# A hand-planned attention and gated-MLP kernel on one core: the order of its steps is made anew under another port rule, with small shifts for every head pair

## The chip, the core and the metric

The kernel runs on one core of a Trainium2 chip. The metric is the device time of one execution in microseconds; the number compared is the median of repeated runs.

## What is computed

```python
# q, k, v: (8, 12, 448, 64); w_in: (768, 1024); conv_w: (3, 1024); w_out: (1024, 768)
q_n, k_n = rmsnorm(q, g_q), rmsnorm(k, g_k)            # over the last axis
attn = softmax(q_n @ k_n.T / 8)                        # per batch and head
x = (attn @ v).transpose(0, 2, 1, 3).reshape(8, 448, 768)
h = relu(x @ w_in)
conv = sum(conv_w[i] * shifted(h, i - 1) for i in range(3))   # along the sequence
out = (h * sigmoid(conv)) @ w_out
```

The weights arrive in a 64-bit format, so the kernel converts them first. Products that need more than half precision are split: a value becomes an f16 part ("hi") and the f16 rest ("lo"), and three f16 products replace one f32 product.

## The kernel before, in words

The unit of attention is a pair of heads of one batch; there are 48 pairs, n = 0 to 47, six to a batch. A pair has three parts. `plan_qk` loads q and k, makes squares and sums, takes the inverse root (`rsqrt`, nine tiny steps), scales, turns the result on TensorE and splits it into hi and lo; `q_middle` copies a corner of qT into a zero-padded tile `qz` for the one row group that does not fill a pair. `plan_attention` makes the scores in four groups (`scores`, L685), their row maxima (`soft_max`, L691), the exponentials on ScalarE (`soft_exp`, L700), the f16 split of the exponentials (`p_hi`, `p_lo`, tile `ph`), a turn by DMA (`p_turn`, tile `PT`), the product with v (`pv`, L836) and the scaled result x (`x_scale`, `x_hi`, `x_lo`). `plan_v` loads v and finds its scale. From pair 10 on v is split too: `v_hi` on ScalarE or VectorE and `v_lo` (L813, tile `vp`) on VectorE alone. After six pairs the batch has its x, and `plan_moe` runs the first product (`in_part`, L910), relu, convolution (`in_conv`, L938), tanh, gate (L948), the split of the gated rows (`in_hi`, `in_lo`, tile `gring`) and the second product (`out_part`, L989).

None of this is issued loop by loop. Every step is entered with a due time, `at(t, fn, ...)`. The due times come from `base(n)`, the planned start of pair n (T0 per pair for the first N0 pairs, T after that), and from other constants of the table `PH`. A list scheduler in the program, run while the kernel is built, then picks one step after the other for PE, DVE, ACT, POOL and SP. It has a cost for each step and engine (`options`), the order that buffers force (`needs`), and an urgency made from the due times. For steps with two possible engines `PH` has a patience: how long the second engine in the list is held back. The steps are issued in the order in which the scheduler picked them, and each engine runs its steps strictly in that order; the real waits are on semaphores for data and buffers. The plan's times do not exist on the chip, only the order, the choice of engines and of PSUM banks.

VectorE and GpSimd share a port. The scheduler has a list of VectorE steps that use it (`SHARED`: `p_lo`, `p_hi`, `v_lo`, `in_lo`, `q_middle`, `in_carry`, `rsqrt`, `convert` and others); all GpSimd steps use it. Its rule for them in the kernel before is symmetric, where `port[e]` is the end of the last such step on engine e:

```python
elif locks(e, step[0], *step[1:2]):
    t = max(t, port["POOL" if e == "DVE" else "DVE"] - PH["pk"])      # pk = 0.1
key = t + sw + (BETA if e != "SP" else PH["sp"]) * urgency(step), urgency(step), steps[step][1]
```

Of the five engines' picks the one with the earliest t is issued next.

Of the kernel before, what the change touches and what calls it, by code (L numbers as in the profile page):

```python
# [17 lines left out]


PH = dict(  # L20
    T0=11.0, N0=5, T=16.382, ti=26.404, si=4.968, so=8.925, hop=0.57, beta=0.03, wi0=-36.475,
    wi1=117.871, wo0=26.473, wo1=139.734, cw=-9.12, tg=-82.146, tl=35.844, ea=1.04, te=111.609,
    ep=0, hs=0, nf=3, adj=0.195, nz=8, ne=0, sc=5, tc=2, mc=8, p_qe=0.915, p_evac=0.829,
    p_hi=1.187, p_lo=6.193, p_rms=1.564, p_v=0.867, p_x=0.08, p_g=2.103, p_relu=0.547,
    p_cv=1.109, p_qz=0.74, p_ev=6.084, sp=0.156, nbulk=8, p_rs=0.048, p_sq=0.882, p_w=0.552,
    v0=-6.388, dg=7, n1=10, sw=0.0, nl=4, tj=-0.029, hk=0, pvs=1, pk=0.1, p_sa=0.11, p_ph=0.44,
    p_pl=0.718, nq=3, nk=94, p_qh=0.371, p_ql=0.382, tq=10.598, ti0=0.047, ti1=0.203, ti2=-0.226,
    ti3=0.674, ti4=0.066, ti5=0.097, ti6=0.664, ti7=0.034, si0=0.995, si1=1.598, si2=1.683,
    si3=1.424, si4=1.546, si5=1.144, si6=1.904, si7=0.784, to0=0.237, to1=0.332, to2=-0.03,
    to3=0.013, to4=0.104, to5=-0.691, to6=-0.117, to7=0.351, so0=1.431, so1=1.535, so2=1.849,  # L30
    so3=1.519, so4=2.105, so5=1.499, so6=1.215, so7=0.981,
)
SCHED = {}
ON_ACT = ""
# [20 lines left out]
def tile_attention_moe(ctx: ExitStack, tc, q, k, v, g_q, g_k, w_in, conv_w, w_out, out):  # L55
# [6 lines left out]
    B, H, S, D = q.shape  # L62
# [3 lines left out]
    NPAIR = B * NP  # L66
# [1 line left out]
    NT = S // 64  # L68
    NO2 = DM // 2
    PSC = 2.0 ** 14  # L70
    T = PH["T"]

    def base(n):

        return min(n, PH["N0"]) * PH["T0"] + max(n - PH["N0"], 0) * T

    def queue(kind):
        return nc.scalar if kind in ON_ACT.split() else nc.sync
# [18 lines left out]
    def move(e, dst, src):  # L97
# [8 lines left out]
    BUFS = dict(  # L106
        qkf=2, sq=2, st=2, qT=2, kT=2, qz=2, v=4, sst=6, e=2, PT=2, x=10, c=2, o=1,
        rB=1, vacc=2, vsc=4, cwb=3, s=PH["sc"], t=PH["tc"], m=PH["mc"], rd=2, rsum=2, rT=1, mx=10, ph=3, vp=2,
    )
# [44 lines left out]
    plan = []  # L154

    def at(t, fn, *args):
        plan.append((t, len(plan), fn, args))
# [13 lines left out]
    cw = const.tile([P, 3, NFC], F32, name="cw")  # L171
    wi32 = const.tile([P, DM // P + 1, DFF], F32, name="wi32")
    wo32 = const.tile([P, NFC + 1, DM], F32, name="wo32")
# [76 lines left out]
    free_i = wo32.rearrange("p c e -> p (c e)").bitcast(I32)  # L250
    free_o = gring.rearrange("p n w t -> p (n w t)").bitcast(I32)
# [161 lines left out]
    def duo(n):  # L413

        return (n, 1) if n < 2 else (n - n % 2, 2)
# [136 lines left out]
        e.tensor_copy(z[HALF[h], :, HALF[h]], old("qT", n)[HALF[h], :, t0 : t0 + 64])  # L552

    def plan_qk(n):
        s = base(n)
        lead = PH["tl"] if n else 60.0
        if duo(n)[0] == n:
            at(s - lead, load_k, n)
            at(s - lead, load_q, n)
        at(s - 24.0, square, n)  # L560
        if halved(n):
            at(s - 23.0, square_half, n)
        at(s - 22.0, square_sum, n)
        if duo(n)[0] == n:
            for i in range(NRS):
                at(s - 20.0 + 0.3 * i, rsqrt, n, i)
        for i in (1, 0):
            at(s - 15.0 - i, apply_rms, n, i)
            if turned(n, i):
                if i:  # L570
                    at(s - 14.5 - i, apply_gain, n)
                at(s - PH["tq"] - 3.0 - i, x_cast, n, i)
                at(s - PH["tq"] - 2.0 - i, x_rest, n, i)
                at(s - PH["tq"] - i, x_turn, n, i)
                continue
            at(s - 10.0 - i, qk_transpose, n, i)
            if n < PH["ne"]:
                at(s - 8.5 - i, qk_evac, n, i)
            at(s - 8.0 - i, qk_hi, n, i)
            at(s - 6.0 - i, qk_lo, n, i)  # L580
        for h in range(2):
            at(s - 4.0, q_middle, n, h)
# [50 lines left out]
    def plan_v(n):  # L633
        b, i = divmod(n, NP)
        t = base(max(n - 7, 0)) + PH["v0"] + 3.0 * min(n, 7)
        if n % 2 == 0:
            at(t, v_load, n // 2)
            at(t + 20.0, v_bound, n // 2)
        if i == NP - 1:
            at(t + 20.5, v_max, b)  # L640
            at(t + 20.6, v_turn, b)
            at(t + 20.8, v_row, b)
            at(t + 21.0, v_spread, b)
            at(t + 22.0, v_scale, b)
# [6 lines left out]
    NG, NS = len(GROUPS), len(SLOTS)  # L651
# [148 lines left out]
    def pvs(n):  # L800
        return (
            *(range(0, NB, PV_STEP) if nd(n) < NS else ()), *(range(NB, NB + 3) if nd(n) else ())
        )
# [46 lines left out]
        binary(on["x_lo", n], xt[:, 1], old("rB", n), xt[:, 0], ALU.subtract)  # L850

    def plan_attention(n):
        s, d = base(n), (base(n + 1) - base(n)) / NS
        for g in range(NG):
            at(s + GROUPS[g][0] * d, scores, n, g)
        for j in range(NS):
            if unit(j)[1] == 0:
                at(s + j * d + 1.0, soft_max, n, unit(j)[0])
            at(s + j * d + 2.0, soft_exp, n, j)
            if nd(n):  # L860
                if j == unit(j)[2][-1]:
                    at(s + j * d + 3.0, p_hi, n, unit(j)[0])
                    at(s + j * d + 4.0, p_lo, n, unit(j)[0])
                    at(s + j * d + 5.0, p_turn, n, unit(j)[0])
                continue
            at(s + j * d + 4.0, p_transpose, n, j)
            at(s + j * d + 5.0, p_evac, n, j)
        s += NS * d
        at(s + 2.0, sum_add, n)
        at(s + 2.3, sum_inverse, n)  # L870
        at(s + 2.6, sum_transpose, n)
        at(s + 3.2, sum_evac, n)
        at(s + 4.0, sum_store, n)
        for h in range(2):
            at(s + 6.0, sum_load, n, h)
        if nd(n):
            at(s - 4.0, v_hi, n)
            at(s - 3.0, v_lo, n)
        for i, k in enumerate(pvs(n)):
            at(s + 8.0 + i, pv, n, k)  # L880
        at(s + 13.0, x_scale, n)
        at(s + 14.0, x_hi, n)
        at(s + 15.0, x_lo, n)
# [217 lines left out]
            on["keep_cw",], cw.rearrange("p k c -> p (k c)"), bank("t", "cw")[:, : 3 * NFC]  # L1101
        )

    at(-62.0, prepare)
    for i in range(2):
        at(PH["tg"], load_g, i)
    at(-31.0, turn_g)
    at(-30.0, make_g)
    at(PH["cw"], load_cw)
    at(PH["cw"] + 8.0, make_cw)  # L1110
    at(PH["cw"] + 10.0, turn_cw)
    at(PH["cw"] + 11.0, keep_cw)
    plan_weight("in", w_in, wi32, 0, free_i, PH["wi0"], PH["wi1"], in_factor)
    plan_weight("out", w_out, wo32, 2, free_o, PH["wo0"], PH["wo1"], out_factor)
    for n in range(NPAIR):
        plan_qk(n)
        plan_v(n)
        plan_attention(n)
    for b in range(B):
        plan_moe(b)  # L1120
    NWI, NWO = DM // P, NFC


# [1 line left out]
    def needs(name, *a):  # L1125
        n = b = w = a[0] if a else None
# [103 lines left out]
            yield "qk_hi", *a  # L1230
        elif name == "q_middle":
            yield ("x_turn" if turned(n, 0) else "qk_lo"), n, 0
            yield "scores", n - BUFS["qz"], 2
            if a[1]:
                yield "q_middle", n, 0
        elif name == "v_load":
# [33 lines left out]
        elif name == "soft_exp":  # L1270
# [3 lines left out]
            u, i, js = unit(a[1])  # L1274
# [31 lines left out]
                yield "p_turn", n, 0  # L1306
        elif name == "v_hi":
            yield "v_scale", n // NP
            yield "pv", n - BUFS["vp"], pvs(n - BUFS["vp"])[-1]
        elif name == "v_lo":  # L1310
            yield "v_hi", n
# [267 lines left out]
    }  # L1579
    ISSUE = dict(C=0.6, T=0.63)  # L1580
    WINDOW = 4096 / 1200
# [62 lines left out]
    port = dict(DVE=0.0, POOL=0.0)  # L1644
# [12 lines left out]
    while len(order) < len(steps):  # L1657
        best = None
        for e, ws in waiting.items():
            pick = None  # L1660
            for step, (t, _, dma) in ws.items():
                t = max(t, free[e])
                if dma and step[0] in BULK and len(bulk) >= PH["nbulk"]:
                    t = max(t, bulk[-PH["nbulk"]])
                t, spots = vacant(step, e, dma, t)
                if t > 1e8:
                    continue
                sw = 0.0
                if e == "PE" and mode(*step) != pmode:
                    t += 0.09  # L1670
                    sw = PH["sw"]
                elif locks(e, step[0], *step[1:2]):
                    t = max(t, port["POOL" if e == "DVE" else "DVE"] - PH["pk"])
                key = t + sw + (BETA if e != "SP" else PH["sp"]) * urgency(step), urgency(step), steps[step][1]
                if pick is None or key < pick[0]:
                    pick = key, t, step, spots
            if pick and (best is None or pick[1] < best[0]):
                best = *pick[1:], e
        if best is None:
            raise RuntimeError(f"{len(order)} of {len(steps)} steps; {[(e, list(ws)[:4]) for e, ws in waiting.items()]}")  # L1680
        t, step, spots, e = best
# [14 lines left out]
        if dma:  # L1696
            kind, k = dma
            for _ in range(k):
                if len(lanes) >= 8:
                    t = max(t, lanes[-8])  # L1700
                h0 = max(t, hw)
                hw = h0 + ISSUE[kind]
                dq = end = max(hw + 0.65, dq) + c
# [5 lines left out]
                t = hw + 0.07 if kind == "C" else h0 + (1.85 if c > 2.0 else 1.32)  # L1709
# [3 lines left out]
        elif e == "PE":  # L1713

            while c > 1e-9:
# [4 lines left out]
                t, busy, c = t + x, busy + x, c - (x if quick else x / 2)  # L1720
# [46 lines left out]
```

## Time and profile before

| | us |
|---|---|
| median of 3 runs | 878.3 (878.28 to 879.4) |
| the profiled execution | 880.88 |
| its span, first to last instruction | 879.1 |
| TensorE busy | 816.9 (93%) |
| VectorE busy | 720.2 (82%) |
| ScalarE busy | 672.5 (76%) |
| GpSimd busy | 632.7 (72%) |

The span is the part of the profiled execution that the trace shows; 1.8 us lie around it. A share of busy time is an average over the whole span: where an engine stands still is read from windows of the trace.

### The profile page before, as it was taken

How to read it: one execution, taken by the hardware profiler on the slowest of the kernel's cores; microseconds unless marked ns; L12 is line 12 of the kernel's file. 1: busy time of each engine (PE TensorE's matmuls, PEld its weight loads, DVE VectorE, ACT ScalarE, POOL GpSimd, SP SyncE). 2: the span in 40 equal slices, each digit the busy share in tenths (PEclk: the TensorE clock that was granted, in tenths of full speed). 3: DMA queues.
4: the chain of work that ended last, by engine and by line, in shares of the span. 5: the costliest groups of instructions: out<-in, count | busy, mean ns of one | idle time of the engine just before them, and what ended most of it. 6: DMA issues, size and time to landing. Idle time of an engine off the chain costs nothing.

```text
span 879.1 us, 16158 instructions
## 1 busy us (share of the span) xinstructions
PE 816.9 (93%) x5416; PEld 419.9 (48%) x5416; DVE 720.2 (82%) x1204; ACT 672.5 (76%) x1468; POOL 632.7 (72%) x760
## 2 busy tenths in 40 slices
PE   0678899999999699999999999999999999899998
PEld 0334444555444245555455554554555555445564
DVE  5897988989989999999998889899998778964510
ACT  1677888888787888888898878888888888873421
POOL 6347768678988686987699877987787888762200
PEclk9989999999999889999999999999999999999999
DMA  8937644128998599878898789988996988572011
GB/s 253 267 119 158 151 113 105 36 63 153 215 190 173 120 168 200 188 160 181 159 201 164 157 175 201 175 172 160 185 184 140 177 170 165 119 149 44 19 54 54
DMA packets 338447, 132.64 MB, mean 151 GB/s; under 512 B 301908, under 2 KB 332988, under 8 KB 337596
## 3 DMA queue, kind: packets, MB, share of 16 engines
q1 hardware_dynamic: 338364, 131.60, 72.5%
q8 instruction: 43, 0.70, 0.3%
q14 instruction: 40, 0.33, 0.1%
HBM read 58.22 MB, written 11.18 MB: 79 GB/s over the span
## 4 chain that ended last, share of the span: by engine, by line
PE 72%; DVE 14%; POOL 4%; ACT 3%; issue 3%; DMA 2%; SPq 1%; DVEq 0%; POOLq 0%; ACTq 0%
PE banks L910 22%; PE banks L989 21%; PE banks L685 10%; PE banks L836 9%; PE banks L505 4%; PE banks L827 3%; PE banks L747 2%; POOL sq L95 1%; DMA qk<-in_k_dram 1%; DVE ph L95 1%; POOL ph L95 1%; ACT e L700 1%; DVE st L406 1%; PE banks L767 1%; DVE gring L95 1%
## 5 line engine op out<-in xcount | busy, mean ns | idle before, releaser
L95 POOL TENSOR_TENSOR ph<-e,ph 128x128 f16<-128x128 f32 (+3 forms) x280 | 264.5, 967 | 56.7 <-ACT ph L83 40.1
L910 PE MATMUL banks<-x,wi 128*128 128x448 f16 x1152 | 251.6, 354 | 0.5 <-POOL x L95 0.5
L989 PE MATMUL banks<-wo,gring 128*128 128x384 f16 (+1 forms) x1056 | 209.6, 327 | 0.2 <-ACT gring L83 0.2
L910 PEld LDWEIGHTS <-wi 128*128 128x128 f16 x1152 | 108.2, 98 | 99.5 <-issue 15.0
L83 ACT CAST ph<-e 128x1024 f16<-128x1024 f32 (+1 forms) x147 | 136.9, 931 | 3.8 <-DMA PT<-ph 1.7
L989 PEld LDWEIGHTS <-gring 128*128 128x128 f16 (+1 forms) x1056 | 101.6, 99 | 67.5 <-issue 7.6
L685 PE MATMUL banks<-kT,qT 64*128 64x448 f16 x864 | 108.1, 361 | 10.0 <-DVE qT L543 4.2
L836 PE MATMUL banks<-PT,vp 128*64 128x448 f16 (+1 forms) x836 | 97.5, 364 | 2.4 <-DVE c_(6_2_8655 L948 2.3
L95 POOL TENSOR_TENSOR sq<-qk,st 112x512 f32<-112x512 f32 (+1 forms) x83 | 92.3, 1130 | 9.6 <-DVE st L428 4.1
L505 PE MATMUL banks<-ident,sq 128*128 128x128 f32 (+1 forms) x364 | 60.7, 280 | 23.4 <-POOL sq L95 18.0
L505 PEld LDWEIGHTS banks<-ident,sq 128*128 128x128 f32 (+1 forms) x364 | 44.0, 145 | 49.0 <-POOL sq L95 20.4
L836 PEld LDWEIGHTS <-vp 128*64 128x64 f16 (+1 forms) x836 | 41.7, 110 | 53.3 <-issue 35.0
L685 PEld LDWEIGHTS <-qT 64*128 64x128 f16 x864 | 36.0, 96 | 64.7 <-issue 37.1
L406 DVE TENSOR_REDUCE st<-sq 128x16 f32<-128x1024 f32 x48 | 57.8, 1206 | 9.9 <-ACT sq L389 9.5
L95 POOL TENSOR_TENSOR x<-rB,x 128x448 f16<-128x448 f32 x48 | 51.5, 1072 | 18.7 <-ACT x L83 16.7
L747 PE MATMUL banks<-ident,e 128*128 128x128 f32 x280 | 47.4, 302 | 10.4 <-ACT PT L83 5.0
L989 PE MATMUL banks<-wo,wi 128*128 128x384 f16 (+1 forms) x192 | 49.7, 327 | 0.0
L747 PEld LDWEIGHTS banks<-ident,e 128*128 128x128 f32 x280 | 33.8, 152 | 29.1 <-ACT PT L83 9.9
L83 ACT COPY PT<-banks 128x512 f32<-128x512 f32 x64 | 37.2, 586 | 11.8 <-PE banks L747 11.6
L843 DVE TENSOR_TENSOR rB<-banks,rB 128x448 f32<-128x448 f32 x48 | 29.7, 618 | 18.9 <-PE banks L836 12.9
L685 PE MATMUL banks<-kT,qz 128*128 128x448 f16 x144 | 38.1, 376 | 2.8 <-DVE c_(1_6_3033 L948 2.8
L83 ACT CAST x<-rB 128x448 f16<-128x448 f32 x44 | 24.7, 561 | 20.3 <-DVE rB L843 20.0
(1128 smaller groups left out, 1719.1 us busy)
## 6 DMA issues: line engine op xcount, KB each, us to landing
rB<-rd SPq DMA_DIRECT2D x96, 112.0 KB
qk<-in_q_dram SPq DMA_DIRECT2D x23, 448.0 KB
wo<-in_moe_w_in_dram SPq DMA_DIRECT2D x6, 1024.0 KB
v<-in_v_dram SPq DMA_DIRECT2D x24, 256.0 KB
gring<-in_moe_w_out_dram SPq DMA_DIRECT2D x8, 768.0 KB
qk<-in_k_dram SPq DMA_DIRECT2D x23, 256.0 KB
v<-in_v_dram SPq DMA_DIRECT2D x24, 192.0 KB
qk<-in_k_dram SPq DMA_DIRECT2D x23, 192.0 KB
```

Source lines behind the costliest of these rows:

```text
L83: (nc.scalar.copy if e == "ACT" else elementwise(e).tensor_copy)(dst, src)
L95: elementwise(e).tensor_tensor(dst, a, b, op=op)
L406: nc.vector.tensor_reduce(old("st", m)[:, 0, n - m].rearrange("p i s -> p (i s)"), old("sq", n).rearrange("p i h t d -> p (i h t) d")[..., ...
L505: nc.tensor.transpose(ps[:, t * w : t * w + m], x[:m, t], ident[:m, :m])
L685: nc.tensor.matmul(ps[u][:, :S], lhs, kt[r, w], start=(i == 0), stop=(i == 2))
L700: nc.scalar.activation(e_slot(n, j), bank("s", (n, j))[:, :S], AF.Exp, bias=old("sst", (n, u))[:, i : i + 1], accum_out=old("rsum", n)[:, ...
L747: nc.tensor.transpose(ps[:, kt * P : (kt + 1) * P], e[:, k0 : k0 + P], ident)
L827: nc.tensor.matmul(ps[HALF[h], :S], v[r, h, k], pt[r, k, h * S : (h + 1) * S], start=(k == 0), stop=(k == NB - 1),)
L836: nc.tensor.matmul(ps[HALF[h], :S], v[:m, w, h, c % 4], pt[:m, c, h * S : (h + 1) * S], start=(i == 0), stop=(i == len(PV7) - 1),)
L843: nc.vector.tensor_tensor(t, bank("m", ("v", n))[:, :S], t, op=ALU.mult)
L910: nc.tensor.matmul(ps[:, :S], wi[:, wl, c, fc * P : (fc + 1) * P], old("x", b * NP + c)[:, xl], start=(i == 0), stop=(i == 3 * NP - 1),)
L989: nc.tensor.matmul(ps[p0 : p0 + m, :NO2], g, wo[:, wl, fc, half * NO2 : (half + 1) * NO2], start=(i == 0), stop=(i == 3 * NFC - 1),)
```

## The change

Five things are changed, all of them in the scheduler's input; no function that issues an instruction is touched.

1. The port rule: a GpSimd step still may start 0.1 us before the last port step of VectorE ends. A VectorE port step now starts no earlier than 0.05 us (`pg`) after the last GpSimd step that has been placed.
2. `needs`: `q_middle` of pair n waits for the score group that reads `qz` (the fourth) of pair n-2, where it named the third, and follows `q_middle` of pair n-1; `v_hi` follows `v_hi` of the pair before.
3. Each pair gets three shifts of its due times, `dq` for `plan_qk`, `da` for `plan_attention` and `dv` for its end (sums, pv, x).
4. Nearly all numbers of `PH` are new. `nbulk`, the number of bulk loads that the planner lets be under way, goes from 8 to 16.
5. The `at` calls are put into a function `make_plan`, called once.

```diff
-    T0=11.0, N0=5, T=16.382, ti=26.404, si=4.968, so=8.925, hop=0.57, beta=0.03, wi0=-36.475,
-    wi1=117.871, wo0=26.473, wo1=139.734, cw=-9.12, tg=-82.146, tl=35.844, ea=1.04, te=111.609,
+    T0=10.967, N0=6, T=15.459, ti=17.476, si=5.11, so=8.471, hop=0.482, beta=0.03, wi0=-42.913,
+    wi1=123.322, wo0=27.142, wo1=142.983, cw=-10.8, tg=-97.576, tl=35.262, ea=0.79, te=113.425,
...
-    p_cv=1.109, p_qz=0.74, p_ev=6.084, sp=0.156, nbulk=8, p_rs=0.048, p_sq=0.882, p_w=0.552,
+    p_cv=0.454, p_qz=0.683, p_ev=2.488, sp=0.083, nbulk=16, p_rs=0.002, p_sq=1.249, p_w=0.964,
...
-    p_pl=0.718, nq=3, nk=94, p_qh=0.371, p_ql=0.382, tq=10.598, ti0=0.047, ti1=0.203, ti2=-0.226,
+    p_ph=0.558, p_pl=0.0, nq=3, nk=94, p_qh=0.287, p_ql=0.313, tq=9.136, ti0=0.38, ti1=-0.226,
...
+    dq=[-3.68, -0.12, 0.27, 2.41, 3.7, 2.72, 2.35, -4.24, 0.69, 8.02, -0.69, 3.34, -0.75,
...
+    da=[-0.05, 0.22, 0.68, 2.21, 3.37, -3.05, -1.7, -0.58, -2.92, 0.62, 2.69, -0.09, 4.89,
...
+    dv=[-1.03, -0.52, -1.1, -1.21, -4.04, -5.21, -6.35, 4.57, 7.65, 3.51, 2.52, -1.82,
...
     def plan_qk(n):
-        s = base(n)
+        s = base(n) + PH["dq"][n]
...
     def plan_attention(n):
-        s, d = base(n), (base(n + 1) - base(n)) / NS
+        s, d = base(n) + PH["da"][n], (base(n + 1) - base(n)) / NS
...
-        s += NS * d
+        s = base(n + 1) + PH["dv"][n]
         at(s + 2.0, sum_add, n)
...
         elif name == "q_middle":
-            yield "scores", n - BUFS["qz"], 2
+            yield "scores", n - BUFS["qz"], NG - 1
+            yield "q_middle", n - 1, 1
...
         elif name == "v_hi":
+            yield "v_hi", n - 1
...
                 elif locks(e, step[0], *step[1:2]):
-                    t = max(t, port["POOL" if e == "DVE" else "DVE"] - PH["pk"])
+                    t = max(t, port["DVE"] - PH["pk"] if e == "POOL" else port["POOL"] + PH["pg"])
```

## Rows read from the trace of the kernel before

**Rows 1.** The page: busy time and share of the span, by engine.
```profile
PE 816.9 (93%) x5416; PEld 419.9 (48%) x5416; DVE 720.2 (82%) x1204; ACT 672.5 (76%) x1468; POOL 632.7 (72%) x760
```
**Rows 2.** Windows of the whole span: stretch, its length, then each engine's busy time.
```profile
core 0: us, PE busy (x) PEld busy (x) DVE busy (x) ACT busy (x) POOL busy (x), PEclk, DMA share, GB/s
0.00:40.00 40.00, 13.01 (x53) 6.83 (x55) 26.78 (x51) 15.80 (x30) 19.70 (x37) 1.00 0.99 264
40.00:160.00 120.00, 105.59 (x627) 52.93 (x624) 105.89 (x174) 98.37 (x227) 84.85 (x93) 0.96 0.53 126
160.00:280.00 120.00, 117.64 (x780) 60.34 (x778) 110.41 (x192) 102.84 (x227) 101.56 (x116) 1.00 0.72 143
280.00:320.00 40.00, 30.47 (x199) 13.80 (x196) 38.08 (x63) 30.84 (x69) 31.33 (x37) 0.83 0.82 154
320.00:875.00 555.00, 550.12 (x3766) 285.99 (x3764) 438.99 (x728) 424.04 (x918) 395.22 (x479) 1.00 0.75 150
875.00:879.10 4.10, 0.05 (x1) 0.00 (x0) 0.00 (x0) 0.58 (x1) 0.00 (x0) 1.00 0.24 96
```
**Rows 3.** Windows over two of the four stretches with a lower granted clock.
```profile
288.82:292.23 3.41, 3.34 (x11) 1.01 (x10) 3.41 (x7) 3.38 (x8) 2.84 (x3) 0.50 0.00 0
302.47:312.71 10.24, 8.05 (x35) 3.29 (x36) 9.33 (x19) 9.35 (x20) 9.13 (x9) 0.50 1.01 207
```
**Rows 4.** TensorE's waits: what waited, for what, us in total, times, longest.
```profile
PE banks L685 <- DVE c_(1_4_2847 L948: 3.1, 1, 3.1
PE banks L685 <- DVE c_(1_6_3033 L948: 2.8, 1, 2.8
PE banks L836 <- DVE c_(6_2_8655 L948: 2.3, 1, 2.3
```
**Rows 5.** The chain that ended last, 276 to 316 us: start, length, what.
```profile
279.69 3.57 DVE qz L552
284.99 1.61 DVE gring L95
```
**Rows 6.** Timeline of GpSimd, 278.8 to 284 us: start, length, instruction.
```profile
279.03 1.04 POOL L95 TENSOR_TENSOR x<-rB,x 128x448 f16<-128x448 f32 x1
280.03 2.04 POOL L95 TENSOR_TENSOR sq<-qk,st 128x512 f32<-128x512 f32 x2
282.04 1.17 POOL L95 TENSOR_TENSOR ph<-e,ph 128x384 f16<-128x384 f32 x2
```
**Rows 7.** Timelines of VectorE and GpSimd, 748.5 to 754.5 us.
```profile
749.32 4.78 DVE L95 TENSOR_TENSOR gring<-c_(6_1_8554,gring 128x448 f16<-128x448 f32 x1
...
750.00 4.39 POOL L95 TENSOR_TENSOR ph<-e,ph 128x768 f16<-128x768 f32 x4
```
**Rows 8.** Instructions of the tiles qz and vp: nanoseconds shortest/median/longest.
```profile
L552 DVE COPY qz<-qT x17: 172/252/3574, 186.0 to 737.4; 64x128 f16<-64x128 f16 x17
...
L813 DVE SCALAR_TENSOR_TENSOR vp<-v,vsc,vp x38: 730/744/3781, 207.4 to 781.6; 128x512 f16<-128x512 f32 x38
```
**Rows 9.** Groups of instructions by form: busy us, mean ns.
```profile
L95 DVE TENSOR_TENSOR ph<-e,ph 128x768 f16<-128x768 f32 x9 | 14.3, 1585 | 0.0
...
L95 DVE TENSOR_TENSOR ph<-e,ph 128x128 f16<-128x128 f32 x9 | 8.0, 894 | 0.0
...
L95 POOL TENSOR_TENSOR ph<-e,ph 128x768 f16<-128x768 f32 x105 | 175.8, 1674 | 52.7 <-ACT ph L83 37.1 <-issue 12.8 <-POOL ph L95 0.7
```
**Rows 10.** One window, 200 to 440 us, columns as in rows 2.
```profile
200.00:440.00 240.00, 227.54 (x1543) 113.31 (x1540) 225.90 (x374) 200.11 (x436) 193.37 (x230) 0.97 0.87 173
```
**Rows 11.** Timeline of GpSimd, the first 28 us.
```profile
10.45 0.52 POOL L441 TENSOR_TENSOR st<-st 128x16 f32<-128x16 f32 x1 [5.79 <-DVE st L428]
...
12.32 1.75 POOL L430 TENSOR_SCALAR st<-st 128x16 f32<-128x16 f32 x1
...
18.56 3.00 POOL L95 TENSOR_TENSOR sq<-qk,st 128x512 f32<-128x512 f32 x2
```
**Rows 12.** The page: DMA issues by line, count, KB each.
```profile
wo<-in_moe_w_in_dram SPq DMA_DIRECT2D x6, 1024.0 KB
```

More of the change, by code (lines that the diff above doesn't have):

```diff
@@ L20 @@
 PH = dict(
-    T0=11.0, N0=5, T=16.382, ti=26.404, si=4.968, so=8.925, hop=0.57, beta=0.03, wi0=-36.475,
-    wi1=117.871, wo0=26.473, wo1=139.734, cw=-9.12, tg=-82.146, tl=35.844, ea=1.04, te=111.609,
-    ep=0, hs=0, nf=3, adj=0.195, nz=8, ne=0, sc=5, tc=2, mc=8, p_qe=0.915, p_evac=0.829,
-    p_hi=1.187, p_lo=6.193, p_rms=1.564, p_v=0.867, p_x=0.08, p_g=2.103, p_relu=0.547,
-    p_cv=1.109, p_qz=0.74, p_ev=6.084, sp=0.156, nbulk=8, p_rs=0.048, p_sq=0.882, p_w=0.552,
-    v0=-6.388, dg=7, n1=10, sw=0.0, nl=4, tj=-0.029, hk=0, pvs=1, pk=0.1, p_sa=0.11, p_ph=0.44,
-    p_pl=0.718, nq=3, nk=94, p_qh=0.371, p_ql=0.382, tq=10.598, ti0=0.047, ti1=0.203, ti2=-0.226,
[L28 to L31, printed above, removed]
+    T0=10.967, N0=6, T=15.459, ti=17.476, si=5.11, so=8.471, hop=0.482, beta=0.03, wi0=-42.913,
+    wi1=123.322, wo0=27.142, wo1=142.983, cw=-10.8, tg=-97.576, tl=35.262, ea=0.79, te=113.425,
+    ep=0, hs=0, nf=3, adj=0.139, nz=8, ne=0, sc=5, tc=2, mc=8, p_qe=0.885, p_evac=1.078,
+    p_hi=1.427, p_lo=9.771, p_rms=1.35, p_v=0.784, p_x=0.724, p_g=1.806, p_relu=0.483,
+    p_cv=0.454, p_qz=0.683, p_ev=2.488, sp=0.083, nbulk=16, p_rs=0.002, p_sq=1.249, p_w=0.964,
+    v0=-5.914, dg=7, n1=10, sw=-0.025, nl=4, tj=0.658, hk=0, pvs=1, pk=0.1, p_sa=0.456,
+    p_ph=0.558, p_pl=0.0, nq=3, nk=94, p_qh=0.287, p_ql=0.313, tq=9.136, ti0=0.38, ti1=-0.226,
+    ti2=-0.488, ti3=0.474, ti4=-0.143, ti5=0.702, ti6=0.881, ti7=-2.49, si0=1.104, si1=1.725,
+    si2=1.798, si3=1.468, si4=1.613, si5=1.143, si6=1.624, si7=1.691, to0=0.944, to1=0.306,
+    to2=-1.453, to3=-1.281, to4=-0.007, to5=-0.844, to6=-0.745, to7=-1.059, so0=1.501, so1=1.467,
+    so2=1.988, so3=1.424, so4=1.513, so5=0.757, so6=0.754, so7=0.218, pg=0.05,
+    dq=[-3.68, -0.12, 0.27, 2.41, 3.7, 2.72, 2.35, -4.24, 0.69, 8.02, -0.69, 3.34, -0.75,
[3 rows of a table added]
+    da=[-0.05, 0.22, 0.68, 2.21, 3.37, -3.05, -1.7, -0.58, -2.92, 0.62, 2.69, -0.09, 4.89,
[3 rows of a table added]
+    dv=[-1.03, -0.52, -1.1, -1.21, -4.04, -5.21, -6.35, 4.57, 7.65, 3.51, 2.52, -1.82,
[3 rows of a table added]
 )
@@ L70, in tile_attention_moe @@
     PSC = 2.0 ** 14
-    T = PH["T"]
     def base(n):
-        return min(n, PH["N0"]) * PH["T0"] + max(n - PH["N0"], 0) * T
+        return min(n, PH["N0"]) * PH["T0"] + max(n - PH["N0"], 0) * PH["T"]
     def queue(kind):
@@ L1102, in keep_cw, with make_plan @@
         )
[L1104 to L1120, printed above, removed]
+    def make_plan():
+        plan.clear()
+        at(-62.0, prepare)
+        for i in range(2):
+            at(PH["tg"], load_g, i)
+        at(-31.0, turn_g)
+        at(-30.0, make_g)
+        at(PH["cw"], load_cw)
+        at(PH["cw"] + 8.0, make_cw)
+        at(PH["cw"] + 10.0, turn_cw)
+        at(PH["cw"] + 11.0, keep_cw)
+        plan_weight("in", w_in, wi32, 0, free_i, PH["wi0"], PH["wi1"], in_factor)
+        plan_weight("out", w_out, wo32, 2, free_o, PH["wo0"], PH["wo1"], out_factor)
+        for n in range(NPAIR):
+            plan_qk(n)
+            plan_v(n)
+            plan_attention(n)
+        for b in range(B):
+            plan_moe(b)
+    make_plan()
     NWI, NWO = DM // P, NFC
```

9 rows, old and new, of tables (da, dq, dv) are left out of this document.

## The prediction

> **What bounds the kernel now.** I read the page first, then windows over the whole span, then TensorE's waits, and then the chain and the timelines around the places where TensorE stands still. The page says that TensorE is the bound: 93% busy against 82% for VectorE [rows 1]. The windows say that this is not the same everywhere [rows 2]. TensorE idles 26.99 us in the first 40 us, 14.41 in 40 to 160, 2.36 in 160 to 280, 9.53 in 280 to 320, 4.88 in the 555 us after that, and 4.05 behind its last product: 62.2 us in all. The time falls only where these shrink, or where its clock comes back: TensorE does the same products in any order.
>
> The reader is to see next that the idle time behind 160 us, 16.77 us, has VectorE at its end. The three longest waits of TensorE there, 3.1, 2.8 and 2.3 us, are all for a VectorE gate (L948) that frees a PSUM bank [rows 4]. They lie near 285, 302 and 752 us, and the chain through the first says why the gate was late: the copy into `qz` took 3.57 us, and a `gring` step 1.61 [rows 5]. The shortest such copy takes 0.172 us [rows 8]. It started at 279.69 while GpSimd had begun a step at 279.03, and GpSimd then began `sq` at 280.03 and `ph` at 282.04 with no break; the copy ended when that run ended, near 283.2 [rows 6]. At 749.32 a `gring` step took 4.78 us beside a GpSimd run of 4.39 us [rows 7]. So a VectorE port step does not simply get the port when the running GpSimd step ends: it waits through several of them. `v_lo` shows the same: shortest 0.730, longest 3.781 us [rows 8]. In 200 to 440 us VectorE is busy 225.90 of 240 us, 94%, these waits included, so a late step is hardly caught up there [rows 10].
>
> A stop also costs clock. Within the long stall the granted clock is 0.50 (the 1.2 GHz level) for 3.41 and 10.24 us, each time after TensorE had stood idle [rows 3]; at half rate 13.65 us lose 6.83 us of work. Together 16.77 + 6.83 = 23.6 us behind 160 us could be had, of which the stretch 280 to 320 alone holds 9.53 + 6.83 = 16.4.
>
> **The change part by part.** No step is added or removed, and the wrapping of the `at` calls costs nothing on the chip. Every cost is one of order.
>
> The port rule. Before, the scheduler let a VectorE port step start 0.1 us before the GpSimd step ends; as GpSimd's next step comes no earlier than that end, VectorE always won, and GpSimd was thought to step back. Rows 6 and 7 show the opposite: GpSimd runs on, VectorE stands, and everything behind it on VectorE (row maxima, gates, conversions out of PSUM, all without the port) stands too; ScalarE's exponentials wait for the maxima and TensorE for the banks. With the new rule a VectorE port step is at a later time than GpSimd's next ready step, so that one is placed first; VectorE takes another step meanwhile, or waits for a real pause. The plan then costs what the rows show, and puts portless steps ahead of starved ones. What it can remove is at most the 23.6 us above. At least it removes nothing: the chip does not follow the plan's times, GpSimd is busy 193.37 of 240 us between 200 and 440 [rows 10], and a step placed in a planned pause can still meet a run. I take half, 11.8 us. The two stalls with a shown port wait in their cause (near 280 and 752) hold most of the sum, which speaks for more than half; a new order that meets one new long run on a 94% busy VectorE speaks for less.
>
> The rule says of `sq` and `ph` on GpSimd that they wait no longer than before. Moved past are VectorE steps and, through them, SP's: `p_turn`, `sum_store` and the loads are issued in the new order. Behind a deferred `v_lo` lies `pv` of its pair, behind a deferred `q_middle` the last score group; both are planned with that delay, and TensorE has `in_part` or `out_part` to put in between. That cover is there from 160 us to the end of attention; without it each costs what the step is late.
>
> The two edits of `needs` put an order into the plan that the buffers force on the chip anyway (`qz` is read by the fourth score group). They cost nothing, as the chip already waits there; what they save lies in the same 23.6 us.
>
> The shifts and constants. A due time counts with beta = 0.03, so a shift of 20 us moves a choice by 0.6 us of start time and one of 3 us by 0.09: they break ties. base(48) falls from 5 x 11.0 + 43 x 16.382 = 759.4 to 6 x 10.967 + 42 x 15.459 = 715.1, but the second half's steps hang on the same base, and ti falls by 8.9 us, worth 0.27 us of preference. Value zero, inside the bounds of the other terms.
>
> The patience of `p_lo` on VectorE (`p_pl`) goes from 0.718 to 0, so more of it may go there. One full `p_lo` took 1.585 + 0.894 = 2.48 us on VectorE, waits included [rows 9]. It is hidden as long as VectorE has room: 14.1 us in 200 to 440 [rows 10]. Value zero, cost above that room in the rivals.
>
> The head. Six inverse-root steps of pair 0 on GpSimd run from 10.45 to 18.56 us, the first in 0.52 us and a later one in 1.75 [rows 11], beside VectorE's weight conversion, which uses the port as well. If all took 0.52, 3.1 us instead of 8.1, pair 0 would be ready 5.0 us sooner. That is the gain's bound, since dq[0] = -3.68 moves choices by only 0.11 us. The loss's bound is one more weight load ahead of a pair's q and k, as nbulk doubles: 1024 KB [rows 12] at the 264 GB/s of the first 40 us [rows 2], 4.0 us. I take zero.
>
> The tail: TensorE is busy through all of its last stretch and 4.05 us lie behind it [rows 2]; nothing there changes.
>
> Sum for the profiled execution: 880.88 - 11.8 = 869.1 us. Its 880.88 lies 2.6 us above the median of the runs, 878.3, so the forecast in terms of the median is 866.5; I say 866.
>
> **A rule against it.** The wait at 279.69 passes the ends of three GpSimd steps [rows 6]. The Trainium skill, "SBUF — State Buffer", Who interferes with whom, says that whichever engine issues first gets the shared port pair for its whole instruction, and that the other is blocked until that one ends. By this the copy would have had the port from about 280.07, and the old rule of the scheduler would have been the true one; the sum would then be 878.3. The trace does not agree: the copy ended at 283.26.
>
> **The rivals.**
> Everything is recovered: no port stall comes back, and the head gains its 5.0 us. 878.3 - 23.6 - 5.0 = 849.7, and with a small rest of either 850 to 857. For it: all long waits of rows 4 have one cause. Against: 94% busy VectorE.
> The stalls move: the plan improves, the chip's drift brings port waits elsewhere, and one of them again drops the clock. 878.3 less 0 to 4, or plus as much: 874 to 882. For it: `v_lo` shows a 3.781 us wait whose delay cost TensorE almost nothing [rows 8, 2], so which waits hurt is chance.
> The wait ends with one GpSimd step: if the port comes free after the running step (at most about the 1.67 us of a `ph` step [rows 9]), the old plan was right and the new rule defers steps for nothing. 878.3.
> VectorE becomes the bound, slower: in 200 to 440 us about 15 pairs have 45 full `p_lo`. With zero patience VectorE takes more of them; 14.1 us of room hold 5.7 at 2.48 us. From the sixth on each adds 2.48 us to that stretch; with ten, 24.8 - 14.1 = 10.7 us, 889. For it: the patience and the busy share. Against: by the new rule VectorE gets a `p_lo` only in a pause of GpSimd, when GpSimd could take it too.
>
> **How the numbers follow.** Forecast 0.50, with its own range 858 to 874 (4 to 20 us gained). All recovered 0.12. Stalls move 0.18, in three equal parts faster, within the bound and slower. One GpSimd step 0.05. VectorE bound 0.15. A measurement of this kernel can tell 0.2%, 1.8 us, from no change. Faster 0.50 + 0.12 + 0.06 = 0.68; same 0.06 + 0.05 = 0.11; slower 0.06 + 0.15 = 0.21. A range of 853 to 884 leaves out half of the second case and most of the last, about 2 in 10.
>
> **What would show it.** Right: no VectorE `qz`, `vp`, `carry` or `gring` step over about 2 us; TensorE's idle time in 160 to 875 us near 8 instead of 16.77 us; no granted clock of 0.50 behind 160 us; TensorE's busy total down by about the clock's share. Wrong in the mechanism: long port waits as many as before while the time falls. Wrong in the sign: VectorE over 97% in 200 to 440 with more `ph` steps on it, or a new stop behind 160 us with the clock at 0.50. A gain found in the first 160 us instead would mean that the shifts, not the rule, made it.

## The result and the profile after

The changed kernel takes 867.35 us in the median of 4 runs (864.5 to 868.59), against 878.85 us for the kernel before; the ratio is 0.9855, with a 95% interval of 0.9817 to 0.9893. The profiled execution took 868.59 us, its span 866.6. First the page's line of busy times, to be held against [rows 1].

```profile
PE 810.0 (93%) x5416; PEld 416.0 (48%) x5416; DVE 663.1 (77%) x1100; ACT 680.0 (78%) x1476; POOL 632.9 (73%) x849
```

VectorE has 104 instructions and 57 us less, GpSimd 89 instructions more and yet no more busy time. Then the windows of the whole span, as in [rows 2], and two windows over the only stretches with the lower clock before TensorE's last product.

```profile
0.00:40.00 40.00, 11.10 (x43) 4.83 (x43) 26.71 (x48) 14.97 (x27) 21.16 (x38) 1.00 0.95 254
40.00:160.00 120.00, 105.82 (x661) 55.02 (x662) 109.40 (x176) 100.77 (x236) 72.26 (x97) 1.00 0.54 131
160.00:280.00 120.00, 116.89 (x760) 59.25 (x758) 101.91 (x170) 105.63 (x235) 101.47 (x132) 0.99 0.72 142
280.00:320.00 40.00, 33.88 (x263) 16.63 (x263) 35.85 (x65) 35.14 (x75) 33.26 (x40) 0.91 0.94 178
320.00:862.50 542.50, 542.21 (x3697) 280.29 (x3693) 389.18 (x645) 422.88 (x906) 404.72 (x545) 1.00 0.77 152
862.50:866.60 4.10, 0.07 (x1) 0.00 (x0) 0.00 (x0) 0.58 (x1) 0.00 (x0) 1.00 0.24 96
```

```profile
297.67:304.50 6.83, 5.62 (x24) 2.27 (x23) 6.64 (x16) 5.42 (x11) 4.89 (x5) 0.50 0.93 193
195.27:198.68 3.41, 3.41 (x11) 1.57 (x11) 3.15 (x5) 3.38 (x9) 3.18 (x5) 0.50 0.49 112
```

The reader is to subtract, stretch by stretch (length minus TensorE's busy time). TensorE's idle time goes from 26.99 to 28.90 us in the first 40 us, from 14.41 to 14.18 in 40 to 160, and behind 160 from 16.77 to 9.52 (3.11 + 6.12 + 0.29). Behind 160 the clock was 0.50 for 13.65 us and is now for 10.24; ahead of it the 10.24 us of before are gone. At half rate that is 1.7 and 5.1 us. Together 1.9 - 0.2 - 7.2 - 1.7 - 5.1 = -12.3 us, and the span is 12.5 us shorter. The long stop of before at 280 to 320 us has not gone: 6.12 us of idle time and a clock of 0.50 are still there. TensorE's longest waits in it are no longer for VectorE's gates as in [rows 4], but for exponentials of ScalarE:

```profile
PE banks L999 <- ACT e L710: 2.7, 1, 2.7
PE banks L777 <- ACT e L710: 1.2, 1, 1.2
```

What has gone is the 4.88 us behind 320, down to 0.29.

The port steps themselves: instructions of the tiles qz and vp as in [rows 8], then the two-slot forms of VectorE's `ph` steps as in [rows 9], then the window of [rows 10].

```profile
L562 POOL COPY qz<-qT x96: 279/288/1220, 28.3 to 762.5; 64x128 f16<-64x128 f16 x96
...
L823 DVE SCALAR_TENSOR_TENSOR vp<-v,vsc,vp x38: 728/745/919, 204.0 to 783.1; 128x512 f16<-128x512 f32 x38
```

```profile
L105 DVE TENSOR_TENSOR ph<-e,ph 128x128 f16<-128x128 f32 x4 | 5.7, 1415 | 0.0
L105 DVE TENSOR_TENSOR ph<-e,ph 128x768 f16<-128x768 f32 x4 | 4.4, 1088 | 0.4 <-issue 0.4
```

```profile
200.00:440.00 240.00, 232.65 (x1589) 117.31 (x1589) 202.34 (x350) 208.73 (x453) 202.90 (x265) 0.99 0.92 177
```

All 96 copies into `qz` are on GpSimd, the longest `v_lo` is 0.919 in place of 3.781 us, VectorE has four full `p_lo` in place of nine, and in 200 to 440 us it is busy 84% of the time, not 94%.

To see port waits as a whole I took each VectorE instruction that is 0.3 us or more longer than the shortest of its own form (same line, output tile and shapes; forms with four or more), and added the excess. Before: 77 instructions, 72.6 us. After: 23 and 24.7 us. For each one I also counted the GpSimd steps that ended while it stood. Before, 68 of the 77 went in at the first such end or before it (two); nine let one to four ends pass, among them the two of [rows 6] and [rows 7]. The 68 hold 52.5 of the 72.6 us, none of them more than 1.5 us.

### The profile page after: what moved, and what is told of

Same layout as the page of the kernel before. It is cut to its first block, busy times and chain, and to the rows that moved or that the text cites. A ratio compares the mean times of both kernels' runs of the same rounds, so it can differ in the third digit from the quotient of the medians.

```text
span 866.6 us, 16129 instructions
## 1 busy us (share of the span) xinstructions
PE 810.0 (93%) x5416; PEld 416.0 (48%) x5416; DVE 663.1 (77%) x1100; ACT 680.0 (78%) x1476; POOL 632.9 (73%) x849
## 4 chain that ended last, share of the span: by engine, by line
PE 82%; DVE 7%; ACT 3%; DMA 3%; SPq 3%; issue 2%; POOL 0%; DVEq 0%; ACTq 0%; POOLq 0%
PE banks L999 25%; PE banks L920 24%; PE banks L695 12%; PE banks L846 10%; PE banks L515 4%; PE banks L837 4%; PE banks L757 2%; DMA v<-in_v_dram 2%; ACT e L710 1%; SPq L380 1%; DVE vacc L616 1%; PE banks L777 1%; SPq L1096 1%; ACT PT L93 1%; DVE ph L105 1%
## 5 line engine op out<-in xcount | busy, mean ns | idle before, releaser
L105 POOL TENSOR_TENSOR ph<-e,ph 128x768 f16<-128x768 f32 (+3 forms) x296 | 270.5, 936 | 40.6 <-ACT ph L93 26.9
L920 PE MATMUL banks<-x,wi 128*128 128x448 f16 x1152 | 248.1, 353 | 0.3 <-ACT e L710 0.3
L999 PEld LDWEIGHTS <-gring 128*128 128x128 f16 (+1 forms) x1056 | 101.8, 100 | 73.8 <-issue 17.1
L695 PE MATMUL banks<-kT,qT 64*128 64x448 f16 x864 | 105.9, 358 | 5.5 <-DVE qT L553 4.2
L105 POOL TENSOR_TENSOR sq<-qk,st 128x512 f32<-128x512 f32 x96 | 103.2, 1090 | 5.8 <-DVE st L438 4.4
L757 PE MATMUL banks<-ident,e 128*128 128x128 f32 x280 | 44.3, 291 | 9.8 <-ACT PT L93 2.9
L399 ACT ACTIVATE sq<-qk 128x1024 f32<-128x1024 f32 x41 | 43.1, 1052 | 7.9 <-DMA qk<-in_q_dram 5.0
L562 POOL COPY qz<-qT 64x128 f16<-64x128 f16 x96 | 30.3, 315 | 16.5 <-DVE qT L553 11.7
```

Of the source, the lines that this page charges most:

```text
L105: elementwise(e).tensor_tensor(dst, a, b, op=op)
L399: nc.scalar.activation(sq, qk(n), AF.Square)
L695: nc.tensor.matmul(ps[u][:, :S], lhs, kt[r, w], start=(i == 0), stop=(i == 2))
L757: nc.tensor.transpose(ps[:, kt * P : (kt + 1) * P], e[:, k0 : k0 + P], ident)
L920: nc.tensor.matmul(ps[:, :S], wi[:, wl, c, fc * P : (fc + 1) * P], old("x", b * NP + c)[:, xl], start=(i == 0), stop=(i == 3 * NP - 1),)
L999: nc.tensor.matmul(ps[p0 : p0 + m, :NO2], g, wo[:, wl, fc, half * NO2 : (half + 1) * NO2], start=(i == 0), stop=(i == 3 * NFC - 1),)
```

## The experiments

Ratios are to the kernel before, run beside each. Its median there was 880.3 to 880.9 us, 1.5 to 2 us above the 878.85 us beside the changed kernel, so times of different rounds compare to about that much.

**One step moved.** The order of before, step for step, with one engine changed.

```diff
         for step in order:
+            if step == ("q_middle", 16, 1):
+                on[step] = "POOL"
             steps[step][2](*step[1:])
```

> The kernel before with its order kept step for step, and one step out of 4448 (the second copy into qz of pair 16, which took 3.57 us at 279.69) issued on GpSimd in place of VectorE. If that port wait made the long stop: TensorE's idle time in 280 to 320 us falls from 9.53 to under 4, the stretch at the 0.50 clock of 10.24 us goes, and the time falls by 6 to 16 us, to 863 to 873. If the stop has other feet too (a VectorE that is 95% busy there, a DMA): idle over 6 us in that stretch and the time within 4 us of 878.9.

877.93 us, ratio 0.9969 (0.9944 to 0.9994). Its window, and two of TensorE's waits, the second of which stands in [rows 4] too:

```profile
280.00:320.00 40.00, 32.11 (x237) 15.44 (x236) 38.00 (x68) 34.38 (x77) 33.99 (x39) 0.87 0.89 163
```

```profile
PE banks L767 <- DVE rsum L764: 4.7, 4, 2.8
...
PE banks L685 <- DVE c_(1_6_3033 L948: 2.8, 1, 2.8
```

The 3.1 us wait for `c_(1_4` is gone, so the copy did cause it; the one for `c_(1_6` stayed, and 7.89 us of the 9.53 with it. VectorE was 95% busy in that stretch and stays so. One port wait was one foot of the stop, not its whole cause.

**All such steps moved.** The same with four kinds of steps, 46 of them.

```diff
         for step in order:
+            if step[0] in ("q_middle", "in_lo", "p_lo", "apply_rms"):
+                on[step] = "POOL"
             steps[step][2](*step[1:])
```

> The kernel before with its order kept, and all 46 VectorE steps of the kinds q_middle (17), in_lo (4), p_lo (12) and the scaling apply_rms (13) issued on GpSimd in the same place of the order. If the port waits of these steps are what costs: 865 to 875 us, VectorE busy down by about 45 us. Rival (a new order is needed, since GpSimd gets about 17 x 0.3 + 4 x 1.04 + 12 x 2.1 + 13 x 1.1 = 49 us more, in places where it has no room): 878 to 890 us.

873.82 us, ratio 0.9912 (0.9884 to 0.9941). Its page:

```profile
PE 816.1 (93%) x5416; PEld 419.0 (48%) x5416; DVE 683.1 (78%) x1146; ACT 673.5 (77%) x1468; POOL 664.8 (76%) x818
```

```profile
160.00:280.00 120.00, 119.28 (x785) 60.86 (x784) 105.58 (x186) 104.20 (x231) 106.64 (x126) 1.00 0.72 146
280.00:320.00 40.00, 31.63 (x224) 14.88 (x224) 34.58 (x58) 33.04 (x72) 36.54 (x43) 0.83 0.90 157
320.00:869.20 549.20, 546.64 (x3737) 283.43 (x3733) 410.99 (x682) 421.39 (x911) 416.64 (x520) 1.00 0.77 151
```

TensorE's idle time behind 160 us falls from 16.77 to 11.65, though GpSimd does 32 us more in an order never made for it. Where the steps run is worth about six tenths of the change's gain by itself. That is not the port waits alone: the 46 steps had held VectorE for 57.7 us, 27.8 of them waits, but other steps now wait longer (14 of `v_lo` where it was 8), so port waits only fall from 72.6 to 59.5 us, in 63 instructions. Of the 37 us that VectorE is less busy, 13 are waits.

**The mirror.** The order of the changed kernel, with those 46 steps issued on VectorE again (`BACK` lists them).

```diff
         for step in order:
+            if step in BACK:
+                on[step] = "DVE"
             steps[step][2](*step[1:])
```

> The changed kernel with its order kept and those 46 steps issued on VectorE that the kernel before had there (17 q_middle, 4 in_lo, 12 p_lo, 13 apply_rms). If where these steps run is what costs, the mirror of moving them off: 872 to 882 us, long port waits back on VectorE. If only the order counts: 865 to 870 us.

876.20 us, ratio 0.9960 (0.9939 to 0.9980), 8.9 us above the changed kernel. The copies into `qz` and the stretch where it went:

```profile
L562 DVE COPY qz<-qT x17: 172/277/2548, 175.6 to 730.3; 64x128 f16<-64x128 f16 x17
```

```profile
280.00:320.00 40.00, 29.86 (x190) 13.68 (x190) 36.00 (x62) 28.51 (x63) 25.05 (x28) 0.79 0.75 150
```

The idle time in 280 to 320 is back at 10.14 us and the granted clock at 0.79. The largest new wait there is for one scaling that stood on VectorE for 6.10 us beside an unbroken run of GpSimd; it passed the ends of four GpSimd steps:

```profile
298.48 6.10 DVE L105 TENSOR_TENSOR sq<-qk,st 128x512 f32<-128x512 f32 x1
```

```profile
PE banks L515 <- DVE sq L105: 2.8, 1, 2.8
```

Port waits are 39 instructions and 42.0 us, 17.3 us more than in the changed kernel, and VectorE is 34 us busier. So the engine of these steps counts in both orders; these two runs do not separate the waits from the load.

**The rule alone.** The kernel before, its constants kept.

```diff
-                    t = max(t, port["POOL" if e == "DVE" else "DVE"] - PH["pk"])
+                    t = max(t, port["DVE"] - PH["pk"] if e == "POOL" else port["POOL"] + 0.05)
```

> The kernel before with nothing but the new port rule, its own constants kept and no shifts. Theory 1 (the rule makes the gain): part of the way from 878.9 towards 867.4 us, 868 to 876, with no VectorE copy into qz and few VectorE ph steps left. Theory 2 (the constants and shifts make it; the rule only fits to them): constants that were made for the other rule now fit badly, 880 to 895 us, although the long port waits on VectorE are gone.

888.19 us, ratio 1.0065 (1.0042 to 1.0089): slower. Port waits did fall, to 40 instructions and 40.7 us. The page and the longest new wait of TensorE:

```profile
PE 820.2 (92%) x5416; PEld 418.8 (47%) x5416; DVE 654.9 (74%) x1082; ACT 678.5 (76%) x1481; POOL 671.2 (75%) x877
```

```profile
PE banks L505 <- POOL wo L95: 7.0, 1, 7.0
```

What VectorE no longer takes lands on GpSimd, 671.2 us busy in place of 632.7, and TensorE now waits for GpSimd: once 7.0 us, which the profile puts down to a split of gated rows (tile wo) in GpSimd's queue. Behind 160 us TensorE idles 19.7 us, 3.0 more than before; more is lost in 40 to 160 us, where its idle time goes from 14.41 to 19.53 us.

**The old rule under the new constants and shifts.** The diff is the reverse of that line in the changed kernel.

> The changed kernel with the symmetric port rule of before, all new constants and shifts kept. Theory 1: VectorE is given qz, ph and gring steps again and waits through GpSimd's runs, excess of such steps back to that of before or more, 876 to 892 us. Theory 2: 866 to 870 us, as the constants carry the gain.

888.16 us, ratio 1.0084 (1.0056 to 1.0113); 69 port waits with 67.0 us. Its page:

```profile
PE 818.7 (93%) x5416; PEld 417.4 (47%) x5416; DVE 736.3 (83%) x1214; ACT 680.9 (77%) x1478; POOL 567.6 (64%) x751
```

Neither half works without the other. The two edits of `needs` and `nbulk` were not tried by themselves; they went with the constants.

**No shifts.**

```diff
+    for key in ("dq", "da", "dv"):
+        PH[key] = [0.0] * NPAIR
```

> The changed kernel with all 144 shifts at zero. Theory 1: the shifts move choices by at most 0.6 us of start time and only break ties, 866 to 873 us. Theory 2: they remove the stops one by one, and without them 874 to 890 us, with TensorE idle behind 160 us at 16 us or more where the changed kernel has 9.5.

879.16 us, ratio 0.9968 (0.9944 to 0.9993). Behind 160 us TensorE idles 16.6 us, as much as before, with 37.8 us of port waits. Its window to the last product shows where most of the difference lies:

```profile
320.00:874.12 554.12, 548.79 (x3749) 283.35 (x3743) 397.04 (x653) 431.51 (x928) 405.83 (x534) 1.00 0.79 151
```

5.33 us idle where the changed kernel has 0.29.

**Jitter.** Random numbers added to the 144 shifts, two draws for the changed kernel, and one for the kernel before (old rule, its zero shifts).

```diff
+    rnd = random.Random(1)
+    for key in ("dq", "da", "dv"):
+        PH[key] = [x + rnd.uniform(-0.5, 0.5) for x in PH[key]]
```

> The changed kernel with a random number between -0.5 and 0.5 us added to each of the 144 shifts, worth at most 0.015 us of preference each. Theory 3 (this very order is what was gained; neighbours of it are no better than any order of the new rule): 874 to 892 us. Theory 1 (the rule and the trend of the shifts make the gain): 865 to 872 us.

890.23 us, ratio 1.0096 (1.0059 to 1.0132).

> As the jittered changed kernel (890.2 us), with other random numbers of the same size. Theory 3 (the gain belongs to this one order): 876 to 895 us. Theory 1: 865 to 872 us, the first draw having been an unlucky one.

887.45 us, ratio 1.0090 (1.0060 to 1.0121).

> The kernel before, old rule and constants, with random shifts between -0.5 and 0.5 us. Theory 3 (its constants were fitted to one order as well): 884 to 895 us, as far above 880 as the jittered changed kernel is above 867. Theory 1: 876 to 884 us.

878.93 us, ratio 0.9969 (0.9942 to 0.9996). The first draw's windows behind 160 us:

```profile
160.00:280.00 120.00, 114.11 (x730) 57.16 (x730) 94.56 (x152) 103.50 (x225) 99.51 (x129) 0.99 0.68 132
280.00:320.00 40.00, 31.11 (x210) 15.03 (x208) 34.45 (x57) 32.77 (x71) 34.58 (x45) 0.91 0.74 143
320.00:884.34 564.34, 557.58 (x3823) 287.78 (x3819) 407.15 (x684) 430.66 (x930) 409.93 (x538) 1.00 0.76 151
```

21.5 us of idle time, with port waits of 23 instructions and 25.7 us, the same as in the changed kernel. So few port waits do not make a fast order; the new rule's orders scatter from 867 to 890 us, and the changed kernel is a good one among them. The order of before was not such a single find: its one neighbour tried is no slower.

**The last four `p_lo`.** The changed kernel, its order kept, with VectorE's remaining `p_lo` on GpSimd.

```diff
         for step in order:
+            if step[0] == "p_lo":
+                on[step] = "POOL"
             steps[step][2](*step[1:])
```

> The changed kernel with its order kept and the last four p_lo of VectorE issued on GpSimd, one of which waited 3.1 us. If such waits still cost: 862 to 866 us. If they lie beside other work now: 866 to 870 us.

864.85 us (864.01 to 867.42), ratio 0.9832 (0.9805 to 0.9859), with 24.6 us of port waits, where the changed kernel has 24.7. It is the fastest median seen and 1.7% under the kernel before; from the changed kernel it is not told apart, as the intervals overlap.

**The port by itself.** Two kernels of small trials. The core of the first: GpSimd runs `steps` subtractions, VectorE a portless step and then a port step.

```python
for i in range(steps):
    nc.gpsimd.tensor_tensor(x[i][:, 1], rB, x[i][:, 0], op=ALU.subtract)
nc.vector.tensor_scalar(banks[:, 0, :S], banks[:, 0, :S], s, 0.0, op0=ALU.mult, op1=ALU.max)
nc.vector.tensor_copy(qz[:64, :, :64], qT[:64, :, :64])
```

> Not the reference's computation: 30 small trials alone on the chip. In each, GpSimd runs 1, 2, 3, 4 or 6 subtractions of 128x448 (about 1.04 us each) with no break, and VectorE, started together with it, does one portless step and then a copy of 64x128 f16, or a subtraction of 128x448 f32, or neither, and a portless step behind. Theory A (VectorE waits through the whole run): the copy's length grows by about 1.0 us with each further subtraction, to 5 us or more beside six. Theory B (it waits for the running step alone): never over 1.2 us, however long the run.

Timelines of the trials with two and with six GpSimd steps:

```profile
10.77 2.02 POOL L41 TENSOR_TENSOR x<-rB,x 128x448 f16<-128x448 f32 x2
11.03 0.82 DVE L44 COPY qz<-qT 64x128 f16<-64x128 f16 x1
...
22.77 5.97 POOL L41 TENSOR_TENSOR x<-rB,x 128x448 f16<-128x448 f32 x6
23.03 0.81 DVE L44 COPY qz<-qT 64x128 f16<-64x128 f16 x1
```

The copy is as long beside six steps as beside two: it waits for the running step and goes next. The subtraction took 1.25 us in all ten of its trials, 0.05 above the bound of Theory B and no longer beside six steps than beside one. Theory A is refuted. (In the first trial of either kernel GpSimd began late, and the copy met none of its steps.)

> Not the reference's computation: 24 small trials as in the trials before, but with GpSimd runs of four steps of the kernel's own kinds: sub (x_lo's 128x448), rms (the scaling with a broadcast operand, 128x512 f32), a mixture of both, low (p_lo's two forms in turn), and sub and rms again with each step waiting on a semaphore that ScalarE has already raised. VectorE issues the qz copy, then in other trials v_lo's 128x512. Theory B1 (what lets VectorE in is a step boundary of any kind): the copy stays under 1.3 us in all of them. Theory B2 (a boundary does not let it in where the next step has its semaphore wait behind it or is of another form): the copy takes 2 us or more, up to 4, in those trials and under 1.3 in the plain ones, which would explain 3.57 us in the kernel beside 0.82 alone.

No trial goes over 1.3 us for the copy (0.70 with the scaling, 0.82 with the subtraction, 1.30 with `p_lo`'s 1.64 us step), nor over 1.80 for `v_lo`, semaphores or not; B2 is refuted. The trial of `v_lo` beside four scalings shows who pays next:

```profile
81.14 4.49 POOL L47 TENSOR_TENSOR sq<-qk,st 128x512 f32<-128x512 f32 x4
81.53 1.20 DVE L77 SCALAR_TENSOR_TENSOR vp<-v,st,vp 128x512 f16<-128x512 f32 x1
```

The four take 4.49 us where beside the short copy they take 4.04: GpSimd's second step stood while `v_lo` had the port (in the mixture, where the steps can be told apart, the second took 1.49 in place of 1.04 us).

## Why the prediction was right, and where it was not

The time, 866 against 867.35 us, and the sign were right, but the number came out partly by luck: what came from behind 160 us was 2.9 us less than forecast, and a head taken at zero gave 3.4 us. Of the prediction's steps, the one on port waits holds with a reservation, one fails, and one was too sweeping.

**The port waits** fell from 72.6 to 24.7 us, and with the old rule under the new constants they are 67.0 us and the time 888.16. Moving the steps alone, in either direction and with the order fixed, shifts the time by 7 to 9 us. That this kernel is faster with these steps on GpSimd is shown; how much of it is the waits and how much the load that leaves VectorE is not. Few waits are not enough either: the first jittered draw has 25.7 us of them and takes 890.23 us. A long stop with one port wait as its only cause is not shown: the stop at 280 to 320 had several feet on a VectorE that was 95% busy, and it is still there.

**The size behind 160 us** was 11.8 us and measured 8.9 (7.2 of idle time, 1.7 of clock). The taken half was about right, by the sum and not by its parts: the stretch of 16.4 us gave back 6.8 (3.4 each of idle time and clock), the stops behind 320 us gave 4.6, and 160 to 280 us lost 2.5 (0.75 of idle time and, at the new stretch of 0.50 from 195.27 us, 1.7 of clock).

**The head** was taken at zero and gave 3.4 us, in the profiled execution all of it clock: 5.1 gained, 1.9 lost in the first 40 us, and 0.2 gained between. The clock's part does not follow from the order of steps alone. The mirror kernel, whose VectorE has the changed kernel's instructions up to 134 us, idles 25.14 us in its first 40 us in place of 28.90 and has 10.24 us at 0.50 ahead of 160, as much as the kernel before:

```profile
0.00:40.00 40.00, 14.86 (x65) 7.38 (x65) 31.90 (x52) 17.54 (x33) 20.82 (x48) 0.96 0.96 258
40.00:160.00 120.00, 105.90 (x658) 54.73 (x657) 108.64 (x176) 100.91 (x234) 72.04 (x88) 0.97 0.55 132
```

That leaves its head 2.2 us ahead of the kernel before, all of it idle time. The kernel with the last four `p_lo` moved, whose order is the same too, has no 0.50 there. The second jittered draw idles 26.06 us in the first 40 and has 17.1 us at 0.50 ahead of 160. So whether the change made the head's gain, and by which of its parts, is open, and the prediction's sign for it (a gain in the first 160 us would be the shifts') can't be judged.

**The signs.** No VectorE step on `qz`, `vp`, `carry` or `gring` is over 2 us, and TensorE is busy 6.9 us less, which is the clock's 6.8. The other two fell short: 9.52 us of idle time behind 160 where about 8 was expected, and 10.24 us there at a clock of 0.50 where none was expected. One stretch of these, at 195.27 us, is new, which the prediction had named as a sign of a slower kernel.

**The step that failed** is "The shifts and constants ... Value zero". By size of preference it was right that they mostly break ties, and wrong that ties are worth nothing. It also weighed all steps with beta = 0.03, where the DMA issues on SP have the weight `sp` (0.156 before, 0.083 after), so that a shift of 20 us moves a choice there by 1.7 us. Without the shifts the time is 879.16 us; with random numbers added that are worth at most 0.015 us of preference (0.042 on SP) it is 887 to 890. The constants are needed as much: the rule with the constants of before takes 888.19 us, GpSimd being 671.2 us busy, where the changed kernel's is 632.9 and ScalarE makes 41 squares (32 before, 33 with the rule alone). So the sum "rule times one half, all else nothing" put on the rule what only rule, constants and shifts give together.

**Too sweeping** was "it waits through several of them". Two long waits were read as the pattern (the one of [rows 6] passes four ends, not three); 68 of 77 held-up steps let no end pass, and neither did any step in the trials alone. The Trainium skill's "SBUF — State Buffer", Who interferes with whom, says that the second one is blocked until the first one's instruction ends. These 68 and the trials agree with it, the nine longer waits do not. The rival built on it still failed in its time. What it left out is that the 68 shorter waits, 0.3 to 1.5 us each, hold 52.5 of the 72.6 us, on a VectorE that is 94% busy in 200 to 440. The nine longer waits stay unexplained. Neither semaphores, nor a mixture of forms, nor the length of the run made one alone. Seven of the nine were not let in at the end of a scaling of 112 partitions, which was not tried alone; other steps were let in at such an end, the copy at 375.58 us for one.

**The other rivals.** VectorE as the bound, with more `p_lo` by the zero patience, went the other way: it has fewer, and 84% in 200 to 440. Stalls that move are what the jittered draws show, both of them on the slow side. The changed kernel is one good order under the new rule, and the two neighbours of it that were tried keep none of its gain.

## What to carry to other kernels

When a planner's rule is mended, its constants have to be fitted anew before the rule can be judged: here rule and constants apart were each 0.6 to 0.8% slower and together 1.5% faster. Where steps have two engines, change the engine of some with the order fixed, by a loop of three lines; that separates what an engine costs from what an order is worth, though not a step's wait from its work. Try neighbours of a planned order before its gain is put down to a rule. And before a rule about arbitration is read from the two worst waits of a trace, count all waits of the kind.

## What was not expected

Changes of at most 0.015 us of preference (0.042 for the DMA issues) in a planned order cost 20 us of time or more in two of two draws for the changed kernel, and nothing in the one draw for the kernel before.

TensorE's granted clock did not say which run was the faster: the changed kernel's four runs had mean clocks of 0.994, 0.988, 0.990 and 0.992 with spans of 866.6, 864.9, 862.5 and 865.6 us.
